# Talking-heads attention: three score tiles instead of two, values block by block with three head pairs an op, zero rows by transfer

## The chip, the cores and the metric

The kernel runs on one core of a Trainium2 chip. The metric is the device time of one execution in microseconds, as the median of several runs. Times inside an execution come from one profiled execution.

## What is computed

Attention over 4 batches, 12 heads, 448 positions and a head dimension of 64, in which the scores of all heads are mixed before the softmax and the weights after it; then two token-wise layers on the result. In short:

```python
scores = scale * np.matmul(q, k.transpose(0, 1, 3, 2))
scores = np.einsum('bhij,hg->bgij', scores, w_pre)
attn = softmax(scores)                      # over j
attn = np.einsum('bhij,hg->bgij', attn, w_post)
x = np.matmul(attn, v)                      # (4*448, 768) after a transpose
h = x @ w_in;  x = (h * np.cos(h)) @ w_out
h = np.maximum(np.maximum(x @ w1, x @ w2), x @ w3)
out = h @ w_out2
```

## The kernel before

The queries of a batch are cut into four **blocks** of 10, 12, 12 and 11 **slots** (the last batch in another order); a slot is 10 query rows, and the 12 heads of those 10 rows make 120 rows that the head mix works on. There are 16 blocks and 180 slots. A block goes through these steps (names and lines are those of the kernel before):

- **scores**: for each of the six head pairs, `qk` (L554) multiplies q and k of two heads on TensorE into two PSUM banks; `evac` (L462, the helper `copy`) copies each head's scores to SBUF, on ACT or DVE, into one of 7 places `s` (the first block uses places of `e` too).
- **regrouping**: `send` (L568) is one DMA a head, SBUF to SBUF, issued on SP. It spreads a head's 100 to 120 rows over the block's tile `t` (a *grid*), so that the 12 heads of a row come to lie on neighbouring partitions. There are two grids; block n uses grid `n % 2`, and a grid is free again when the block two earlier has been mixed. Four partitions of each grid are never written by a send and have to be zero; `fill` (L500) clears them with one GpSimd memset a grid.
- **mix and softmax**: a *visit* is two slots. `mix1` (L577) mixes heads on TensorE into two banks, `rowmax` (L585, DVE) and `soft` (L591, ACT) follow, then three small DVE steps, then `mix2` (L615) mixes the weights on TensorE into two banks of the pool `ps_t`, and `keep` (L462) copies each to the tile `a2`.
- **values**: blocks are grouped in **halves** (`HALVES`, L27): in batches 1 and 2 the halves are the blocks of 10 and 12 slots and those of 12 and 11; batches 0 and 3 have two halves of a single block and one of two. `av` (L641, L644) multiplies `a2` of a half with v, two head pairs an op, in one bank of `ps_t`; `keepx` (L462) copies each pair's part of each block to a tile `xs`, and `out` (L658) is one DMA a pair to `xT` in DRAM. `ps_t` has two banks, which mix2 and av share.

After attention the two layers run on TensorE (L158 to L160, three matmuls for each float32 product). Their input `x` (L141) is read back from `xT` into a tile of the same ring as the grids; the first few of their matmuls run between the last visits.

The order on every engine is fixed when the kernel is built: `Plan.run` (L392) takes the steps by modelled start time and rank, with modelled durations, rings of places and landing times. Each engine then works through its own list in that order; so does the SP queue with its DMAs.

```python
r = (first[n - 1] - 2.5 + 0.1 * score[n - 1][3] * hp) if n else -40.0 + hp   # L687: rank of block n's scores
```

Of the kernel before, what the change touches and what calls it, by code (L numbers as in the profile page):

```python
# [9 lines left out]
F32 = mybir.dt.float32  # L10
# [6 lines left out]
B, H, S, D = 4, 12, 448, 64  # L17
# [11 lines left out]
NHALF = 230  # L29
# [416 lines left out]
def attention(ctx, tc, q, k, v, w_pre, w_post, same_row, xT, tp, mlps):  # L446
# [34 lines left out]

    score, halves = [], []
    for b, sizes in enumerate(HALVES):
        i = 0
        for n, half in enumerate(sizes):
            start, column, nhalf = min(i, S - RI * half[0]), 0, len(halves)
            for slots in half:
                i = min(i, S - RI * slots)
                score.append((b, i, RI * slots, slots, nhalf, column))
                column += RH * slots  # L490
                i += RI * slots
            halves.append((b, start, i - start, 2 * column, range(len(score) - len(half), len(score))))
    visits = [(n, t, range(min(2, x[3] - t))) for n, x in enumerate(score) for t in range(0, x[3], 2)]
# [5 lines left out]
    def fill(n, _):  # L499
        nc.gpsimd.memset(grids[n][:PAD], 0.0)  # L500

# [64 lines left out]
    def send(n, h, eng):  # L566
        slots = score[n][3]
        queue_of[eng].dma_start(grids[n % 2][PAD + h:PAD + RI * H:H, :slots, :], live.pop(("s", n, h))[:RI * slots])  # L568

    def mix1(v, _):  # L570
        n, t, slots = visits[v]
        for a in range(2):
            live["m", v, a] = ps_m.tile([128, S], F32, name="mps")
        for y in slots:
            for a in range(2):
                k = slice(64 * a, PAD + (a + 1) * PH)
                nc.tensor.matmul(live["m", v, a][64 * y:64 * y + 64], w1[k], grids[n % 2][k, t + y, :],  # L577
                                 start=True, stop=True)
# [39 lines left out]
    def keep(v, y, eng):  # L618
        n, t, _ = visits[v]
        half, o = score[n][4], score[n][5] + RH * (t + y)  # L620
        if ("a2", half) not in live:
            live["a2", half] = ap_.tile([128, JB, H, NHALF // 2], F32, name="a2")
        copy(eng, live["a2", half][:, :, :, o:o + RH].rearrange("p u g r -> p (u g) r"),
             live["a", v, y].rearrange("p u (g r) -> p (u g) r", r=RH))


    def pairs(x):
        return 2 * x, 2 * x + 1

    def av(half, x, _):  # L630
        b, _, _, m, _ = halves[half]
        a2, w = live["a2", half], m // 2
        both = ps_t.tile([128, 512], F32, name="aps")
        for n, hp in enumerate(pairs(x)):
            ps = live["av", hp] = both[:, n * NHALF:n * NHALF + m].rearrange("p (a w) -> p a w", a=2)
# [10 lines left out]
    def keepx(half, hp, eng):  # L646

        xs = live["xs", hp] = xp.tile([128, NHALF], F32, name="xs")
        ps = live["av", hp]
        for n in halves[half][4]:  # L650
            _, i0, m, slots, _, c = score[n]
            o = i0 - halves[half][1]
            copy(eng, xs[:, o:o + m].rearrange("p (a r t) -> p a r t", a=2, t=slots),
                 ps[:, :, c:c + m // 2].rearrange("p a (t r) -> p a r t", r=RH))

    def out(half, hp, eng):
        b, i0, m = halves[half][:3]
        queue_of[eng].dma_start(xT[hp * 128:(hp + 1) * 128, b * S + i0:b * S + i0 + m], live["xs", hp][:, :m])  # L658

# [19 lines left out]
    for n in range(2):  # L679
        add(fill, (n,), -60.0, {"P": 5.0})  # L680
    add(wmix, (0,), -39.0, {"V": 0.8}, [("wget", 0), ("wget", 2)])
    add(wmix, (1,), -39.0, {"V": 0.2}, [("wget", 1), ("wget", 2)])
    for n in range(NS):
        b = score[n][0]
        start, end = score[n - 1][0] != b or not n, n == NS - 1 or score[n + 1][0] != b
        for hp in range(HP):
            r = (first[n - 1] - 2.5 + 0.1 * score[n - 1][3] * hp) if n else -40.0 + hp  # L687
            if start:
# [6 lines left out]
            for h in range(2 * hp, 2 * hp + 2):  # L695
                add(evac, (n, h), r, {"A": 0.42, "V": 0.53}, [("qk", n, hp)], turn=True, lands=0.16, takes=[place := copy_place(n, h)[0]], frees=[(ring, ("qk", n, hp), h % 2)])
                if h == 0:
                    plan.add(("new_t", n), r, lambda _: None, {}, [("evac", n, 0)], takes=["t"])
                add(send, (n, h), r, {"D": score[n][2] / 125.0}, [("evac", n, h), ("new_t", n)], turn=True, frees=[(place, ("evac", n, h))], lands=5.0)


    for y, (n, t, slots) in enumerate(visits):
# [12 lines left out]
        for c in slots:  # L715
            begin = n == halves[score[n][4]][4][0] and t == c == 0
            add(keep, (y, c), i + 1.5, {"A": 0.41, "V": 0.51}, [key("mix2")], turn=True, lands=0.17, takes=["a2"] * begin,
                frees=[("ps_t", key("mix2"), c)])


    for half, (b, _, _, _, members) in enumerate(halves):
        last = (first + [N])[members[-1] + 1] - 1
        ylast = starts[members[-1] + 1] - 1
        room = min(12, starts[halves[half + 1][4][-1] + 1] - 1 - ylast) if half + 1 < len(halves) else 12
        ends = [("keep", y, a) for y, x in enumerate(visits) if x[0] in members for a in x[2]]
        start = ends[0]
        for x in range(HP // 2):
            r = last + 2.5 + 3.0 * x
            for hp in pairs(x) if halves[half][1] == 0 else ():
                add(vget, (b, hp), r - 10.0, {"D": 0.8}, [("send", 0, H - 1)], turn=True, takes=["v"], lands=3.0)  # L730
            add(av, (half, x), r, {"T": 0.25 + 0.0139 * halves[half][3]}, [("vget", b, hp) for hp in pairs(x)] + ends, turn=True, takes=["ps_t"],
                frees=[("a2", start)] + [("v", ("vget", b, hp)) for hp in pairs(x) if halves[half][1] + halves[half][2] == S],
                behind=from_visit(ylast + 2 + x * room // 3))
            for hp in pairs(x):
                add(keepx, (half, hp), r, {"A": 0.13 * len(members), "V": 0.18 * len(members)}, [("av", half, x)], turn=True, lands=0.2,
                    takes=["xs"], frees=[("ps_t", ("av", half, x))])
                add(out, (half, hp), r, {"D": 0.5}, [("keepx", half, hp)], turn=True, frees=[("xs", ("keepx", half, hp))], lands=3.0)

# [207 lines left out]
    for n in range(2):  # L946
        r = (r0, N - 1)[n] + RANK[("fx", "x1")[n]]
        add(xget, (n,), r, {"D": 3.6}, [("out", x, hp) for x, y in enumerate(halves) if y[0] == n for hp in range(H // 2)] + [("xget", 0)] * n
            + [("block", FG)], takes=["t"])
# [36 lines left out]
    first_layer(0)  # L986
    plan.add(("open_late",), N, open_late, {}, [("keepx", len(halves) - 1, hp) for hp in range(HP)], behind=att_keys)
    for r, job in sorted(jobs):
# [118 lines left out]
    for u, (l, (j, wi)) in enumerate(units):  # L1107
# [72 lines left out]
    plan.run({**BUFS, "t": 2, "ps": BUFS["ps_x"], "mark": NM, "u": 7,  # L1180
              **{(tag, early): n if early else of - n for tag, (n, of) in PLACES.items() for early in (True, False)}})
# [45 lines left out]
```

## Time and profile before

| | us |
|---|---|
| median of 3 runs | 1140.23 (1139.26 to 1142.84) |
| the profiled execution's own time | 1143.35 |
| its span | 1141.5 |
| TensorE busy, share of the span | 97% |
| DVE busy, share of the span | 85% |
| ACT busy, share of the span | 58% |
| mean share of the 16 DMA engines' time, first 17 of 40 slices | 0.4 to 0.7 |

The steps below are measured against the profiled execution; its own time is 0.27% above the median. TensorE's records overlap, since matmuls are pipelined, so its busy share does not tell how close it is to its limit: what counts is the distance from the start of one group of matmuls to the start of the next. In a timeline row the columns are start, duration, engine, line, operation, `out<-in`, shapes and the count of merged instructions; in brackets stands the engine's idle time before it and what ended it.

### The profile page before, as it was taken

How to read it: one execution, taken by the hardware profiler on the slowest of the kernel's cores; microseconds unless marked ns; L12 is line 12 of the kernel's file. 1: busy time of each engine (PE TensorE's matmuls, PEld its weight loads, DVE VectorE, ACT ScalarE, POOL GpSimd, SP SyncE). 2: the span in 40 equal slices, each digit the busy share in tenths (PEclk: the TensorE clock that was granted, in tenths of full speed). 3: DMA queues.
4: the chain of work that ended last, by engine and by line, in shares of the span. 5: the costliest groups of instructions: out<-in, count | busy, mean ns of one | idle time of the engine just before them, and what ended most of it. 6: DMA issues, size and time to landing. Idle time of an engine off the chain costs nothing.

```text
span 1141.5 us, 28936 instructions
## 1 busy us (share of the span) xinstructions
PE 1112.7 (97%) x11548; PEld 936.5 (82%) x11548; DVE 974.8 (85%) x2060; ACT 661.9 (58%) x1493; POOL 76.7 (7%) x67
## 2 busy tenths in 40 slices
PE   7989999999998999999999999999999999999998
PEld 2556766676667899999999999999999999999987
DVE  4868677887978999999999999997987779778994
ACT  3757666667867885555555555555634354445572
POOL 4000000000023100000000000000001022011120
PEclk8999999999999999999999999999999999999999
DMA  7676685655554654434444444420012111222233
GB/s 227 199 221 199 207 218 158 203 179 155 167 181 139 200 153 139 138 118 131 126 128 128 130 116 125 130 89 22 1 56 76 63 49 41 77 64 69 85 121 113
DMA packets 92903, 146.79 MB, mean 129 GB/s; under 512 B 12288, under 2 KB 75360, under 8 KB 92768
## 3 DMA queue, kind: packets, MB, share of 16 engines
q1 hardware_dynamic: 92512, 144.92, 42.6%
q8 instruction: 91, 1.49, 0.5%
q14 instruction: 44, 0.36, 0.1%
q0 software_dynamic: 256, 0.02, 0.0%
HBM read 85.74 MB, written 20.45 MB: 93 GB/s over the span
## 4 chain that ended last, share of the span: by engine, by line
PE 86%; DMA 5%; DVE 4%; ACT 2%; issue 1%; SPq 1%; POOL 0%; ACTq 0%; DVEq 0%; POOLq 0%
PE ps L158 22%; PE ps L159 22%; PE ps L160 22%; PE aps L615 6%; PE mps L577 6%; PE ps L554 5%; PE aps L641 4%; DMA t<-s 2%; DMA x<-xT 1%; PE aps L644 1%; DMA k<-in_k_dram 1%; ACT e L591 1%; DMA xT<-xs 1%; DMA t<-e 1%; DVE nm L585 0%
## 5 line engine op out<-in xcount | busy, mean ns | idle before, releaser
L158 PE MATMUL ps<-x,w 128*128 128x448 f32 x816 | 300.0, 368 | 0.8 <-ACT gh L869 0.6
L160 PE MATMUL ps<-x,w 128*128 128x448 f32 x816 | 299.1, 367 | 0.3
L159 PE MATMUL ps<-x,w 128*128 128x448 f32 x816 | 299.1, 367 | 0.3 <-DVE w L298 0.3
L158 PEld LDWEIGHTS ps<-x,w 128*128 128x128 f32 x816 | 153.2, 188 | 15.3 <-ACT gh L869 1.0
L160 PEld LDWEIGHTS ps<-x,w 128*128 128x128 f32 x816 | 153.2, 188 | 14.9 <-POOL x L149 1.0
L159 PEld LDWEIGHTS ps<-x,w 128*128 128x128 f32 x816 | 153.2, 188 | 14.0 <-DVE w L298 0.7
L615 PEld LDWEIGHTS aps<-w2s,e 60*64 60x64 f32 x5040 | 103.7, 136 | 49.6 <-issue 25.9
L158 PE MATMUL ps<-gh,w 128*128 128x448 f32 x384 | 140.8, 367 | 0.0
L159 PE MATMUL ps<-gh,w 128*128 128x448 f32 x384 | 140.7, 366 | 0.0
L160 PE MATMUL ps<-gl,w 128*128 128x448 f32 x384 | 140.4, 366 | 0.0
L295 ACT CAST w<-wf 128x384 fp32r<-128x384 f32 x168 | 81.1, 514 | 77.5 <-DVE wf L287 55.8
L585 DVE TENSOR_REDUCE nm<-mps 128x1 f32<-128x448 f32 (+1 forms) x184 | 108.5, 615 | 20.3 <-PE mps L577 19.3
L591 ACT ACTIVATE e<-mps,nm 128x448 f32<-128x448 f32 (+1 forms) x184 | 116.3, 641 | 13.7 <-DVE nm L585 9.7
L615 PE MATMUL aps<-w2s,e 60*64 60x60 f32 x5040 | 105.4, 220 | 8.9 <-DVE xs L462 2.4
L554 PE MATMUL ps<-k,q 64*64 64x448 f32 (+3 forms) x736 | 101.0, 561 | 2.9 <-ACT s L462 2.7
L577 PE MATMUL mps<-t,w 64*64 64x448 f32 (+1 forms) x720 | 95.8, 567 | 7.3 <-DMA xT<-xs 4.6
L826 DVE TENSOR_TENSOR acc<-ps,acc 128x448 f32<-128x448 f32 x168 | 100.5, 617 | 0.6 <-PE ps L160 0.6
L298 DVE TENSOR_TENSOR w<-wf,w 128x384 fp32r<-128x384 f32 x132 | 75.3, 591 | 18.8 <-ACT w L295 18.0
L254 ACT ACTIVATE wf<-wraw 128x384 f32<-128x384 f32 x112 | 61.9, 554 | 48.9 <-DMA wraw<-in_w_out_dram 32.1
L298 POOL TENSOR_TENSOR w<-wf,w 128x384 fp32r<-128x384 f32 x36 | 43.6, 1217 | 674.4 <-DVE wt L258 365.1
L160 PEld LDWEIGHTS ps<-gl,w 128*128 128x128 f32 x384 | 72.1, 188 | 6.5
L158 PEld LDWEIGHTS ps<-gh,w 128*128 128x128 f32 x384 | 72.1, 188 | 6.3
(123 smaller groups left out, 1757.8 us busy)
## 6 DMA issues: line engine op xcount, KB each, us to landing
t<-s SPq DMA_DIRECT2D x96, 210.0 KB
wf<-w SPq DMA_DIRECT2D x96, 192.0 KB
wraw<-in_w_out_dram SPq DMA_DIRECT2D x44, 384.0 KB
wraw<-in_w_dram SPq DMA_DIRECT2D x36, 384.0 KB
wraw<-in_w_in_dram SPq DMA_DIRECT2D x32, 384.0 KB
t<-s SPq DMA_DIRECT2D x48, 192.5 KB
w<-wf SPq DMA_DIRECT2D x48, 192.0 KB
t<-s SPq DMA_DIRECT2D x42, 175.0 KB
```

The source lines that it names most:

```text
L158: mm(w[0], x[0], start=first, stop=False)
L159: mm(w[1], x[0], start=False, stop=False)
L160: mm(w[0], x[1], start=False, stop=last)
L254: nc.scalar.activation(o["f"], f32(o["raw"][:, :, 1]), AF.Abs)
L295: return nc.scalar.copy(A[x][0], w())
L298: return eng.tensor_sub(A[x][1], w(), f32(A[x][0]))
L554: nc.tensor.matmul(live["s", n, 2 * hp + g][r:end], live["q", b, hp][half, i0 + r:i0 + end], live["k", b, hp][half], start=True, stop=True)
L577: nc.tensor.matmul(live["m", v, a][64 * y:64 * y + 64], w1[k], grids[n % 2][k, t + y, :], start=True, stop=True)
L585: nc.vector.tensor_reduce(nm, of(v, live["m", v, a]), axis=AX.X, op=ALU.max, negate=True)
L591: nc.scalar.activation(of(v, e), of(v, live["m", v, a]), AF.Exp, bias=live["nm", v, a], scale=1.0, accum_out=live["z", v][:, a:a + 1])
L615: nc.tensor.matmul(live["a", v, y][64 * c:64 * c + 64, u], live["e", v, a][k, j * JC:j * JC + JC], live["w2s", v][k, a], start=True, stop= ...
L826: return nc.vector.tensor_add(acc, po, acc) if fg else nc.scalar.copy(acc, po)
```

## The change

- There are three grids; the third lies in the attention's constant pool. Block n uses grid n % 3, and the scores of block n get an earlier rank (8.0 instead of 2.5 steps ahead).
- `HALVES` is gone. `av` works on one block, three head pairs an op; `keepx` is one copy an op, of 300 to 360 columns, and `out` one DMA an op. `a2` and `xs` change their sizes; there are 9 places `s` instead of 7 and 3 larger `xs` instead of 6.
- `fill` is a DMA on ACT's queue from a small zeroed tile, one for each grid, instead of GpSimd memsets.
- In the first block the sends of heads 1, 4, 7 and 10 are issued on GpSimd's queue instead of SP's.
- The last batch's blocks have 12, 12, 11 and 10 slots.

```diff
-HALVES = [[[10], [12], [12, 11]], [[10, 12], [12, 11]], [[10, 12], [12, 11]], [[12, 11], [12], [10]]]
+SLOTS = [[10, 12, 12, 11]] * 3 + [[12, 12, 11, 10]]
+PG = 3
-BUFS = {"k": 10, "q": 9, "s": 7, "e": 6, "w2s": 3, "v": 7, "xs": 6, "a2": 2, "ps_m": 4, "ps_t": 2, "ps_x": 2}
+BUFS = {"k": 10, "q": 9, "s": 9, "e": 6, "w2s": 3, "v": 7, "xs": 3, "a2": 2, "t": 3, "ps_m": 4, "ps_t": 2, "ps_x": 2}
...
-    grids = [tp.tile([128, RT, S], F32, tag="t", name="t") for _ in range(2)]
+    grids = [const.tile([128, RT, S], F32, name="t")] + [tp.tile([128, RT, S], F32, tag="t", name="t") for _ in range(2)]
+    none = const.tile([PAD, S], F32, name="none")
+    nc.vector.memset(none, 0.0)
...
     def fill(n, _):
-        nc.gpsimd.memset(grids[n][:PAD], 0.0)
+        nc.scalar.dma_start(grids[n][:PAD], none[:PAD].unsqueeze(1).to_broadcast([PAD, RT, S]))
...
-    def av(half, x, _):
+    def av(n, x, _):
+        b, _, m, _ = score[n]
+        a2, w = live["a2", n], m // 2
+        live["av", n, x] = ps_t.tile([128, 512], F32, name="aps")[:, :PG * m]
+        for y, hp in enumerate(group(x)):
+            ps = live["av", n, x][:, y * m:y * m + m].rearrange("p (a w) -> p a w", a=2)
...
+    def keepx(n, x, eng):
+        m, slots = score[n][2:]
+        xs = live["xs", n, x] = xp.tile([128, PG * RT * RI], F32, name="xs")[:, :PG * m]
+        copy(eng, xs.rearrange("p (a r t) -> p a r t", r=RH, t=slots),
+             live["av", n, x].rearrange("p (a t r) -> p a r t", r=RH, t=slots))
...
-            r = (first[n - 1] - 2.5 + 0.1 * score[n - 1][3] * hp) if n else -40.0 + hp
+            r = (first[n - 1] - 8.0 + 0.1 * score[n - 1][3] * hp) if n else -40.0 + hp
...
-                add(send, (n, h), r, {"D": score[n][2] / 125.0}, ..., lands=5.0)
+                add(send, (n, h), r, {"P": 0.6} if n == 0 and h % 3 == 1 else {"D": score[n][2] / 125.0}, ..., lands=7.0)
```

How the instructions move, in three places. First ACT's list at the start of the program (a number behind a name tells tiles apart; brackets give the semaphores that a row waits for, DMAHW those of DMAs). Before:

```order
L462 ACT_TABLE_LOAD
L462 COPY s_179<-ps_170 100x448 [waits PE_49]
L462 COPY s_193<-aps_185 100x448 [waits PE_49]
L462 COPY s_207<-mps_199 100x448 [waits PE_49]
L462 COPY s_222<-ps_212 100x448 [waits PE_49]
```

and with the change:

```order
L500 DMA t_136<-none_139 4x12x448 [waits DVE_49]
L500 DMA t_137<-none_139 4x12x448 [waits DMAHW5_49]
L500 DMA t_138<-none_139 4x12x448 [waits DMAHW6_49]
L464 ACT_TABLE_LOAD
L464 COPY s_184<-ps_176 100x448 [waits PE_49]
```

Three DMAs now stand ahead of ACT's first copy, and two of them wait for a DMA's semaphore, the ones of the third pair's q and k.

Second, SP's list of DMAs where the first block's sends end. Before:

```order
L568 DMA t<-e 10x10x448
L568 DMA t<-s 10x12x448 x8
L539 DMA v_126<-in_v_dram 64x512 x2
L568 DMA t<-s 10x12x448 x2
L539 DMA v_127<-in_v_dram 64x512 x2
```

and with the change:

```order
L568 DMA t<-e 10x10x448 x2
L568 DMA t<-s 10x12x448 x10
L539 DMA v_126<-in_v_dram 64x512 x2
L568 DMA t<-s 10x12x448 x2
L539 DMA v_127<-in_v_dram 64x512 x2
L539 DMA v_128<-in_v_dram 64x512 x2
L568 DMA t<-s 10x12x448 x6
```

Ten instead of eight sends of the second block (10x12x448) stand ahead of the first loads of v, and six of the third block's follow before the other three loads of v.

Third, PE's list where the values of a block of 12 slots follow a visit. Before, in the half of 12 and 11 slots of batch 0:

```order
L577 MATMUL mps<-t,w_124 64x448 x4
L641 MATMUL aps<-a_1251,v_126 64x230 x6
L644 MATMUL aps<-a_1251,v_126 64x115 x4
L641 MATMUL aps<-a_1251,v_127 64x230 x6
L644 MATMUL aps<-a_1251,v_127 64x115 x4
L641 MATMUL aps<-a_1251,v_128 64x230 x6
L644 MATMUL aps<-a_1251,v_128 64x115 x4
L641 MATMUL aps<-a_1251,v_129 64x230 x6
L644 MATMUL aps<-a_1251,v_129 64x115 x4
L554 MATMUL ps<-k,q 64x448 x2
```

and with the change, the last three of the six head pairs of the block of 12 slots:

```order
L640 MATMUL aps<-a_1266,v_129 64x120 x6
L643 MATMUL aps<-a_1266,v_129 64x60 x4
L640 MATMUL aps<-a_1266,v_130 64x120 x6
L643 MATMUL aps<-a_1266,v_130 64x60 x4
L640 MATMUL aps<-a_1266,v_131 64x120 x6
L643 MATMUL aps<-a_1266,v_131 64x60 x4
L554 MATMUL ps<-k,q 64x448 x2
L554 MATMUL ps<-k,q 56x448 x2
L615 MATMUL aps<-w2s,e 64x60 x28
```

The rows of a head pair are as many as before and half as wide, and all six pairs of the block come in a row.

## Rows read from the trace of the kernel before

**Rows 1.** Busy time by stretch; columns as in the first line.

```profile
core 0: us, PE busy (x) PEld busy (x) DVE busy (x) ACT busy (x) POOL busy (x), PEclk, DMA share, GB/s
24.00:112.00 88.00, 82.20 (x1986) 51.51 (x1987) 70.00 (x186) 58.99 (x161) 0.00 (x0) 0.93 0.73 207
112.00:192.00 80.00, 77.32 (x1873) 54.71 (x1872) 62.95 (x174) 53.37 (x150) 0.00 (x0) 1.00 0.68 195
192.00:272.00 80.00, 77.96 (x1880) 54.08 (x1872) 64.09 (x177) 53.82 (x151) 0.00 (x0) 1.00 0.60 180
272.00:363.00 91.00, 84.55 (x1960) 62.91 (x1956) 73.48 (x182) 62.90 (x169) 14.86 (x13) 1.00 0.54 162
363.00:1141.00 778.00, 773.52 (x3784) 708.88 (x3781) 692.53 (x1325) 424.40 (x851) 48.33 (x40) 1.00 0.34 101
```

**Rows 2.** Timeline of PE, one visit after another in batch 1.

```profile
121.28 1.02 PE L577 MATMUL mps<-t,w 64*64 64x448 f32 x8
...
123.60 1.01 PE L577 MATMUL mps<-t,w 64*64 64x448 f32 x8
```

**Rows 3.** Timeline of PE, values: two neighbouring head pairs at each width.

```profile
113.55 1.34 PE L641 MATMUL aps<-a,v 128*64 128x230 f32 x12
...
115.11 1.34 PE L641 MATMUL aps<-a,v 128*64 128x230 f32 x12
...
338.48 0.80 PE L641 MATMUL aps<-a,v 128*64 128x120 f32 x12
...
339.33 0.80 PE L641 MATMUL aps<-a,v 128*64 128x120 f32 x12
...
44.76 0.76 PE L641 MATMUL aps<-a,v 128*64 128x100 f32 x12
...
45.54 0.72 PE L641 MATMUL aps<-a,v 128*64 128x100 f32 x12
```

**Rows 4.** Timeline of PE, waits within the attention.

```profile
119.76 0.97 PE L615 MATMUL aps<-w2s,e 60*64 60x60 f32 x50 [0.34 <-DVE xs L462]
...
78.08 1.27 PE L554 MATMUL ps<-k,q 64*64 64x448 f32 x8
82.08 1.77 PE L577 MATMUL mps<-t,w 64*64 64x448 f32 x8 [2.74 <-DMA xT<-xs]
...
164.58 0.98 PE L577 MATMUL mps<-t,w 64*64 64x448 f32 x8 [1.82 <-DMA xT<-xs]
```

**Rows 5.** Busy time by stretch of 4 us, columns as in rows 1.

```profile
4.00:8.00 4.00, 3.45 (x18) 0.83 (x16) 2.18 (x4) 0.53 (x1) 4.00 (x5) 1.00 0.96 291
...
20.00:24.00 4.00, 2.56 (x8) 0.28 (x6) 0.00 (x0) 1.06 (x2) 0.00 (x0) 0.50 0.66 205
...
84.00:88.00 4.00, 4.00 (x68) 2.08 (x64) 2.54 (x6) 2.27 (x6) 0.00 (x0) 0.50 0.78 215
```

**Rows 6.** Timeline of all engines, the start of the program.

```profile
1.29 1.20 POOL L510 DMA_DIRECT2D wraw<-in_w_pre_dram  x2 [0.83 <-DVE blk L473]
...
6.54 0.53 ACT L462 COPY s<-ps 100x448 f32<-100x448 f32 x1 [4.51 <-PE ps L554]
...
8.24 0.56 PEld L554 LDWEIGHTS mps<-k,q 64*64 64x64 f32 x8 [0.93 <-DMA q<-in_q_dram]
...
10.63 4.02 DVE L516 TENSOR_SCALAR wraw<-wraw 128x12 f32<-128x12 f32 x1
...
17.53 0.76 SPq L568 DMA_DIRECT2D t<-e  x1
...
24.10 3.27 PE L577 MATMUL mps<-t,w 64*64 64x448 f32 x16 [1.14 <-DMA t<-e]
```

**Rows 7.** Chain of waits, start and length, where the first layer's input is read back.

```profile
320.82 8.56 DMA x<-xT
```

**Rows 8.** Groups of copies on ACT, by shape.

```profile
L462 ACT COPY a<-aps 128x420 f32<-128x420 f32 x94 | 52.7, 563 | 37.2 <-PE aps L615 35.4
...
L462 ACT COPY xs<-aps 128x120 f32<-128x120 f32 x26 | 6.6, 263 | 30.1 <-PE aps L644 30.1
```

More of the change, by code (lines that the diff above doesn't have):

```diff
@@ L479, in attention @@
         nc.tensor.matmul(begun[:64], w1[:64], places[0][:64].rearrange("p j g d -> p (j g d)")[:, :S], start=True, stop=True)
-    score, halves = [], []
-    for b, sizes in enumerate(HALVES):
+    score = []
+    for b, sizes in enumerate(SLOTS):
         i = 0
[L485 to L492, printed above, removed]
+        for slots in sizes:
+            i = min(i, S - RI * slots)
+            score.append((b, i, RI * slots, slots))
+            i += RI * slots
     visits = [(n, t, range(min(2, x[3] - t))) for n, x in enumerate(score) for t in range(0, x[3], 2)]
@@ L619, in keep, with group @@
         n, t, _ = visits[v]
[L620 to L623, printed above, removed]
+        if ("a2", n) not in live:
+            live["a2", n] = ap_.tile([128, JB, H, RT * RH], F32, name="a2")
+        copy(eng, live["a2", n][:, :, :, RH * (t + y):RH * (t + y + 1)].rearrange("p u g r -> p (u g) r"),
              live["a", v, y].rearrange("p u (g r) -> p (u g) r", r=RH))
-    def pairs(x):
-        return 2 * x, 2 * x + 1
-    def av(half, x, _):
[L631 to L635, printed above, removed]
+    def group(x):
+        return range(PG * x, PG * x + PG)
+    def av(n, x, _):
[4 more added lines that the diff above has]
+            ps = live["av", n, x][:, y * m:y * m + m].rearrange("p (a w) -> p a w", a=2)
             for j in (*range(1, JP + 1), 0, JP + 1):
@@ L644, in av, with out @@
                         nc.tensor.matmul(to[:, a], of, rows[:, 2 * JP], start=False, stop=j > 0)
[L646 to L658, printed above, removed]
+    def keepx(n, x, eng):
[3 more added lines that the diff above has]
+             live["av", n, x].rearrange("p (a t r) -> p a r t", r=RH, t=slots))
+    def out(n, x, eng):
+        b, i0, m, _ = score[n]
+        known = max(0, sum(score[n - 1][1:3]) - i0) if n and score[n - 1][0] == b else 0
+        to = xT.rearrange("(c p) t -> p c t", p=128)[:, PG * x:PG * x + PG, b * S + i0 + known:b * S + i0 + m]
+        queue_of[eng].dma_start(to, live["xs", n, x].rearrange("p (c m) -> p c m", m=m)[:, :, known:])
     before = {}
@@ L715, in attention @@
         for c in slots:
-            begin = n == halves[score[n][4]][4][0] and t == c == 0
-            add(keep, (y, c), i + 1.5, {"A": 0.41, "V": 0.51}, [key("mix2")], turn=True, lands=0.17, takes=["a2"] * begin,
+            add(keep, (y, c), i + 1.5, {"A": 0.41, "V": 0.51}, [key("mix2")], turn=True, lands=0.17, takes=["a2"] * (t == c == 0),
                 frees=[("ps_t", key("mix2"), c)])
[L721 to L729, printed above, removed]
-                add(vget, (b, hp), r - 10.0, {"D": 0.8}, [("send", 0, H - 1)], turn=True, takes=["v"], lands=3.0)
[L731 to L737, printed above, removed]
@@ new lines, in attention @@
+    for n, (b, i0, m, slots) in enumerate(score):
+        last = (first + [N])[n + 1] - 1
+        ylast = starts[n + 1] - 1
+        ends = [("keep", y, a) for y, x in enumerate(visits) if x[0] == n for a in x[2]]
+        for x in range(HP // PG):
+            r = last + 2.5 + 4.0 * x
+            for hp in group(x) if i0 == 0 else ():
+                add(vget, (b, hp), r - 10.0, {"D": 0.8}, [("send", 0, H - 1)], turn=True, takes=["v"], lands=3.0)
+            add(av, (n, x), r, {"T": 0.3 + 0.0209 * m}, [("vget", b, hp) for hp in group(x)] + ends, turn=True, takes=["ps_t"],
+                frees=[("a2", ends[0])] + [("v", ("vget", b, hp)) for hp in group(x) if i0 + m == S],
+                behind=from_visit(ylast + 2 + 3 * x))
+            add(keepx, (n, x), r, {"A": 0.1 + 0.0025 * m, "V": 0.08 + 0.003125 * m}, [("av", n, x)], turn=True, lands=0.2,
+                takes=["xs"], frees=[("ps_t", ("av", n, x))])
+            add(out, (n, x), r, {"D": 0.5}, [("keepx", n, x)], turn=True, frees=[("xs", ("keepx", n, x))], lands=3.0)
@@ L947, in attention @@
         r = (r0, N - 1)[n] + RANK[("fx", "x1")[n]]
-        add(xget, (n,), r, {"D": 3.6}, [("out", x, hp) for x, y in enumerate(halves) if y[0] == n for hp in range(H // 2)] + [("xget", 0)] * n
+        add(xget, (n,), r, {"D": 3.6}, [("out", x, y) for x, of in enumerate(score) if of[0] == n for y in range(HP // PG)] + [("xget", 0)] * n
             + [("block", FG)], takes=["t"])
```

15 lines of the change are left out of this document (7 added, 8 removed).

## Prediction

> **What bounds the kernel now.** I read the stretches first, then PE's timeline, then the waits. From 363 us on PE runs the two layers: 773.5 of 778 us busy with 3784 matmuls, 0.204 us each [rows 1]. The changed order has the same 3780 product matmuls in a row there, so this part stays, and the change is worth what it does between 24 and 363 us.
>
> There, busy time tells little; pitches do. A visit (one mix, one score pair, one weight mix) takes 123.60 - 121.28 = 2.32 us from one mix to the next when PE waits for nothing [rows 2], a third of it (0.77) for each. A head pair's values take 115.11 - 113.55 = 1.56 us at 230 columns, 0.85 at 120 and 0.78 at 100 [rows 3]; for 220 I take 1.50 in proportion. A batch has 22.5 visits, 1.5 score pairs more than visits, and two halves of six head pairs: 52.2 + 1.2 + 6 x (1.56 + 1.50) = 71.8 us of work for PE. The stretches of batches 1 and 2, which begin at the same point of their batches, are 80 us long [rows 1], so 8.2 us of each are lost. The first stretch holds, by the order of before, 23.5 full visits, four mixes and 2.5 score pairs more, and twelve narrow head pairs: 54.5 + 4.9 + 9.8 = 69.2 of 88 us; 18.8 are lost. The last one (the whole, 288.2 us of work, less the other three, 36 product matmuls among it) has 75.4 of 91; 15.6 are lost. PE's work is thus 85% of the attention, and 51 us are waits, half clock and switches.
>
> Where they are: mixes that wait for the sends of their block (2.74 us idle at 82.08, and 82.08 - 78.08 - 0.77 = 3.2 us in all; 1.82 at 164.58 [rows 4]; the record named is a DMA to xT, but the mix reads t, and its last send shares that DMA's semaphore); PE at half clock, granted 0.50 at 84 to 88 us after that wait and at 20 to 24 us before the first mix [rows 5]; and weight mixes that wait for a bank while four copies to xs follow each other after a wide op (0.34 us at 119.76 [rows 4], seven such).
>
> **The change, part by part.**
>
> *Third grid, earlier scores, 9 places s.* A send needs about 0.6 us of copy, 0.76 us of issue [rows 6] and, judging by the first block (issued at 17.53, mixed at 24.10 [rows 6]), some 6 us to land: 8 us from the last score to the first mix. Counted in the orders, PE has between the last score pair and the first mix of block 3 two mixes, two weight mixes, three score pairs and four value pairs before: 8.8 us of work. With the change it has six, five, five and six: 17.5 us. So 8.8 us just covers the landing and 17.5 covers it twice. The waits for sends should go: 1.8 us in batch 1 [rows 4]. In the first stretch 18.8 us are lost where batches 1 and 2 would lose 8.2 x 88/80 = 9.0; of the 9.8 above that I leave 3 us, the half clock right after the first mix (about 6 us of work at half speed [rows 5]), and take 6.8 away: the wait at 82.08, the 3 us that its half clock costs, and small ones. What is late next is ACT and DVE: together 116 us busy per 80 us [rows 1], 73% each, if shared evenly.
>
> *Values block by block.* Six wide halves become twelve narrow blocks; all 16 blocks are narrow then: four of 100, four of 110 (0.815, between the others), eight of 120 columns. 6 x (4 x 0.78 + 4 x 0.815 + 8 x 0.85) = 79.1 us against 6 x (4 x 1.56 + 2 x 1.50 + 2 x 0.78 + 2 x 0.85) = 75.0: **+4.1 us**, all on PE. The number of ops hardly changes, 32 for 30.
>
> *One copy an op.* 96 copies of about 0.26 us become 32 of 360 columns or less; between 120 columns (263 ns) and 420 (563 ns) [rows 8] that is 0.5 us. ACT and DVE lose some 9 us of work between them, hidden behind PE. On PE's path is the chain of four copies after a wide op; with one copy of 0.5 us behind a score pair of 0.77 us the bank is free in time: 7 x 0.34 = **-2.4 us**. If the copy queues behind others on its engine, this stays; bounds 0 and -2.4.
>
> *32 DMAs to xT instead of 60*, of rows half as long: nobody waits for them but the read of x. Taken as nothing.
>
> *The read of x.* It waits for the tile of the block two earlier before, and is on the chain with 8.56 us [rows 7]; ACT stands in its list at the cast of x until it lands, and copies for PE queue behind that. With three grids the tile is that of block 13, free a block earlier. The last stretch loses 15.6 us where 9.3 would be usual; bounds 0 and -6.3, and I take **-3**, since that stretch also has no scores left to fill PE, which stays.
>
> *The beginning.* Three things that the trace does not show together. SP issues 8 sends instead of 12 at 0.76 us or more, and both GpSimd memsets go, in whose time a DVE step on 12 columns took 4.02 us [rows 6] with two heads' copies behind it: up to 4 x 0.76 = 3 us earlier. Against it, ACT now has three DMAs ahead of its first copy, the last two behind the landing of the third pair's q and k; PE had waited for that until 8.24, while the first copy began at 6.54 [rows 6]. So ACT begins some 2 to 3.5 us later. And four sends go through GpSimd, whose nearest DMAs, of 60 short rows, took 0.6 us each to issue [rows 6]. Bounds -3 and +3.5; I take 0, as the two large parts are equal and opposite. The second of them is a price of the three zero rows only: 258 KB at 291 GB/s [rows 5] would be 0.9 us.
>
> On that price the row and a rule differ. While q and k were loaded, the DMA engines were 0.96 busy and moved 291 GB/s; with the sends alone in flight, 0.66 and 205 GB/s [rows 5], although PE was waiting for them. The Trainium skill (DMA: Bandwidth & Descriptors, "Why a DMA increments its semaphore by 16 and not by 1") says that a transfer is spread over the largest number of engines up to 16 that divides its outermost dimension: 10 for a send, 4 for a fill. The 0.66, near 10/16, agrees. By that rule the fills take 258 KB at a quarter of 291 GB/s, 3.5 us of four engines that every send also uses, and the sum would be 3 us higher.
>
> *Sum:* -1.8 - 6.8 + 4.1 - 2.4 - 3 + 0 = **-9.9 us**. The profiled execution took 1143.35 us, so 1133.4; it stood 0.27% above the median of 1140.23, against which I forecast **1130**. The bounds of these terms alone give 1124 to 1137.
>
> **The rivals.**
>
> *More than that goes.* If the long lead also empties ACT's and DVE's queues at the right times, batches 1 and 2 lose half (4 us each), the start comes 3 us earlier and the first half clock with it. For: within the visits PE runs at 2.32 us without a gap. Against: 73% of two engines in fixed order seldom leaves no gaps. 1130 - 8 - 6 = 1116.
>
> *The sends do not get ahead.* Scores wait in s until sent; if DMAs with q, k and v of two batches in the same queue limit the first stretch (share 0.73 there [rows 1]), its 6.8 us stay. For: 0.96 at the start. Against: 0.60 to 0.68 in batches 1 and 2. 1137. This is also the case that the change does not do what it says.
>
> *The waits move.* PE is held back by ACT and DVE whichever grid is ready: 51 us stay lost, and the narrow values cost 4.1, the copies give 2.4: 1142.
>
> *A late beginning: slower.* The first mix needs all twelve heads. If the fills hold ACT, its copies hold PE's banks, and the four GpSimd sends are slow to write out (100 rows of 448 values where the trace has 60 of 12), the first mix comes late one for one, and PE idles at half clock meanwhile. From a first mix at 34 us on, 10 us late, the gain is eaten; four sends of 4 us each behind a first copy at 10 us, with 6 us to land, would put it at 32 and the half clock makes it worse. At 44 us it is 1150. For: three DMAs ahead of ACT's copies. Against: 0.6 us an issue.
>
> **How the numbers follow.** A measurement of this kernel tells 0.3%, 3.4 us, from no change. Forecast 0.52 (1124 to 1135); more 0.20 (1112 to 1124); sends not ahead 0.13 (1135 to 1139, half of it faster than the bound); waits move 0.08; late beginning 0.07. Faster 0.80, same 0.13, slower 0.07. For 8 in 10 I leave out the lower end of the second case and the last two but for their edge: 1115 to 1139.
>
> **What would show it.** First mix between 21 and 28 us. No mix of batches 0 to 2 that waits for a send by over 1 us, and no half clock between 35 and 350 us. Value pairs at 0.78 to 0.85 us, copies to xs near 0.5 us, no weight mix waiting for them. x landed before ACT needs it. The end of the attention near 353 us and the rest of 778 us unchanged. I am wrong if the first mix is past 30, if the first batch still takes 88 us, or if batches 1 and 2 take 80 us or more: then ACT and DVE bound them.

## The result

The change made the kernel slower: 1159.41 us (median of four, 1156.19 to 1162.49) against 1139.89 on the same chip, ratio 1.014 (95%: 1.010 to 1.018). The forecast was 1130, with a range of 1115 to 1139. The profiled execution took 1158.15 us, span 1156.0, beside 1143.35 and 1141.5 before.

Busy time by stretch of the changed kernel, columns as in [rows 1]; the last two lines are eight microseconds each of the layers:

```profile
24.00:112.00 88.00, 77.56 (x1734) 50.75 (x1736) 54.78 (x145) 52.79 (x137) 0.00 (x0) 0.91 0.74 217
112.00:192.00 80.00, 78.39 (x2130) 59.30 (x2128) 62.02 (x165) 55.14 (x145) 0.00 (x0) 1.00 0.70 201
192.00:272.00 80.00, 78.86 (x2130) 60.88 (x2126) 57.43 (x156) 57.01 (x153) 0.00 (x0) 1.00 0.62 184
372.17:1156.00 783.83, 776.48 (x3781) 711.01 (x3780) 693.04 (x1322) 423.44 (x847) 49.08 (x41) 1.00 0.33 100
388.00:396.00 8.00, 5.52 (x19) 3.87 (x18) 7.86 (x12) 6.87 (x16) 3.64 (x4) 0.76 0.32 85
396.00:404.00 8.00, 8.00 (x34) 7.26 (x33) 7.97 (x14) 5.50 (x13) 1.62 (x2) 0.81 0.39 118
```

The first stretch has 77.6 us of PE where it had 82.2 [rows 1]; the two whole batches after it are a little fuller. Three points divide the span: the first mix (24.10 before, 31.54 after), the end of the last values (363.15, 372.17) and the end. The 14.5 us of the two spans are +7.4 before the first mix, +1.6 from there to the end of the attention, where the forecast had nearly all its gain, and +5.5 in the layers, where it had nothing.

The beginning, timeline of ACT and PE of the changed kernel:

```profile
1.49 9.79 ACTq L500 DMA_DIRECT2D t<-none  x3
...
12.60 0.53 ACT L464 COPY s<-ps 100x448 f32<-100x448 f32 x1
...
18.25 0.97 PE L554 MATMUL mps<-k,q 64*64 64x448 f32 x8 [1.82 <-DMA k<-in_k_dram]
...
31.54 2.84 PE L577 MATMUL mps<-t,w 64*64 64x448 f32 x16
```

ACT is held for 9.79 us at its three DMAs of zero rows (the second and third wait for the third pair's q and k) and copies from 12.60 on (6.54 before [rows 6]), and a score of block 0 still waits for its k until 18.25. The chain of waits shows why that k is late. With the change it has the first DMA of zero rows, for whose landing a load of k in SP's list waits, and then the last k of block 0:

```profile
1.49 6.80 DMA t<-none
...
9.16 8.96 DMA k<-in_k_dram
```

Before, loads of k stand there, and the last of them on the chain lands 12.6 us after the start:

```profile
2.13 4.75 DMA k<-in_k_dram
6.90 5.72 DMA k<-in_k_dram
```

The first batch, SP's own list, then what waits for it:

```profile
82.11 3.35 SPq L568 DMA_DIRECT2D t<-s  x4
85.51 2.35 SPq L539 DMA_DIRECT2D v<-in_v_dram  x2
...
92.60 2.17 SPq L529 DMA_DIRECT2D k<-in_k_dram  x1
94.86 3.48 SPq L568 DMA_DIRECT2D t<-s  x4
...
100.42 0.62 DVE L464 COPY s<-ps 120x448 f32<-120x448 f32 x1 [7.00 <-DMA t<-s]
...
101.10 1.00 PE L554 MATMUL ps<-k,q 64*64 64x448 f32 x3 [6.54 <-DVE s L464]
```

No mix waits there for more than 0.6 us any more. A score pair of the next block does: its copy needs a place s, the places are full until sends leave, and 9 us of loads and writes (85.51 to 94.86) stand between two sets of sends in SP's list. PE idles 6.54 us and then runs at half clock (0.50 granted from 100 to 104).

The start of the layers, waits on PE's timeline:

```profile
390.05 0.47 PE L162 MATMUL ps<-x,w 128*128 128x448 f32 x1 [0.80 <-DVE x L151]
...
392.51 0.74 PE L160 MATMUL ps<-x,w 128*128 128x448 f32 x1 [1.38 <-ACT x L147]
...
393.91 0.74 PE L162 MATMUL ps<-x,w 128*128 128x448 f32 x1 [0.29 <-POOL x L151]
```

PE waits 2.5 us for the parts of x of the third quarter of the tokens, and the mean granted clock falls to 0.76 and 0.81 for two stretches of 8 us (3.4 us of work). Before, the same place has three short pauses (0.44 to 0.49 us from one start to the next, where 0.2 is usual) and full clock:

```profile
379.00:387.00 8.00, 7.69 (x36) 6.20 (x35) 7.93 (x15) 6.74 (x16) 2.44 (x2) 1.00 0.38 103
387.00:395.00 8.00, 8.00 (x41) 7.41 (x40) 7.97 (x14) 7.15 (x17) 2.30 (x2) 1.00 0.42 127
```

A fourth kind of wait was nearly absent before. PE stops in the middle of a weight mix, for nothing that the profile shows:

```profile
154.37 0.99 PE L615 MATMUL aps<-w2s,e 60*64 60x60 f32 x49
...
156.98 0.34 PE L615 MATMUL aps<-w2s,e 60*64 60x60 f32 x7 [1.61 <-issue]
```

It runs 49 of 56 matmuls, then comes a gap, then the other 7. Such gaps of 0.4 us or more add up to 6.0 us in the attention, 1.2 before.

### The profile page after: what moved, and what is told of

Same layout as the page of the kernel before. It is cut to its first block, busy times and chain, and to the rows that moved or that the text cites. A ratio compares the mean times of both kernels' runs of the same rounds, so it can differ in the third digit from the quotient of the medians.

```text
span 1156.0 us, 30223 instructions
## 1 busy us (share of the span) xinstructions
PE 1119.8 (97%) x12268; PEld 958.2 (83%) x12268; DVE 960.1 (83%) x2012; ACT 667.9 (58%) x1479; POOL 69.0 (6%) x68
## 4 chain that ended last, share of the span: by engine, by line
PE 89%; DMA 5%; DVE 2%; ACT 2%; issue 1%; SPq 1%; POOL 0%; DVEq 0%; POOLq 0%; ACTq 0%
PE ps L160 22%; PE ps L161 22%; PE ps L162 22%; PE aps L615 6%; PE mps L577 6%; PE ps L554 5%; PE aps L640 5%; DMA t<-s 2%; PE aps L643 2%; DMA v<-in_v_dram 1%; DMA k<-in_k_dram 1%; DMA t<-none 1%; DMA wraw<-in_w_in_dram 0%; DVE x L151 0%; POOL x L151 0%
## 5 line engine op out<-in xcount | busy, mean ns | idle before, releaser
L615 PEld LDWEIGHTS aps<-w2s,e 60*64 60x64 f32 x5040 | 107.5, 135 | 40.8 <-issue 14.3
L591 ACT ACTIVATE e<-mps,nm 128x448 f32<-128x448 f32 (+1 forms) x184 | 117.2, 649 | 20.4 <-DVE nm L585 18.3
L585 DVE TENSOR_REDUCE nm<-mps 128x1 f32<-128x448 f32 (+1 forms) x184 | 108.6, 613 | 12.1 <-PE mps L577 11.2
L554 PE MATMUL ps<-k,q 64*64 64x448 f32 (+3 forms) x736 | 105.8, 572 | 10.5 <-DVE s L464 6.5
L464 DVE COPY s<-ps 120x448 f32<-120x448 f32 (+2 forms) x82 | 49.7, 619 | 64.0 <-PE ps L554 51.7
L577 PE MATMUL mps<-t,w 64*64 64x448 f32 (+1 forms) x720 | 99.9, 555 | 1.3 <-issue 0.6
```

The source lines that it names most:

```text
L554: nc.tensor.matmul(live["s", n, 2 * hp + g][r:end], live["q", b, hp][half, i0 + r:i0 + end], live["k", b, hp][half], start=True, stop=True)
L585: nc.vector.tensor_reduce(nm, of(v, live["m", v, a]), axis=AX.X, op=ALU.max, negate=True)
L591: nc.scalar.activation(of(v, e), of(v, live["m", v, a]), AF.Exp, bias=live["nm", v, a], scale=1.0, accum_out=live["z", v][:, a:a + 1])
L615: nc.tensor.matmul(live["a", v, y][64 * c:64 * c + 64, u], live["e", v, a][k, j * JC:j * JC + JC], live["w2s", v][k, a], start=True, stop= ...
```

## The experiments

All runs are in one table. It gives the ratio to the kernel before on the same chip (95% interval; where there is one run alone, its time and before's median) and, from one profile each and in us, the start of the first mix, the end of the attention, the time from there to the end (layers) and the sum of PE's gaps without visible cause in the attention. Ten runs of one kernel (e1) spread over 1143.9 to 1154.8, so a difference of a few us between two single profiles proves nothing by itself.

| kernel | ratio | first mix | attention ends | layers | gaps |
|---|---|---|---|---|---|
| before | 1 | 24.1 | 363.2 | 778.4 | 1.2 |
| changed | 1.014 (1.010–1.018) | 31.5 | 372.2 | 783.8 | 6.0 |
| e1 old beginning | 1.0046 (1.0013–1.0080) | 26.3 | 364.1 | 782.3 | 6.5 |
| e2 before, new beginning | 1.0067 (1.0031–1.0103) | 27.7 | 368.4 | 779.4 | 1.9 |
| e3 old fills, new sends | 1.0061 (1.0027–1.0094) | 29.7 | 364.8 | 781.8 | 5.2 |
| e4 before, values by block | 1.0090 (1.0058–1.0123) | 21.5 | 368.1 | 787.2 | 11.2 |
| e5 DMA fills, old sends | 1153.2 / 1145.4 | 31.3 | 370.0 | 781.3 | 7.5 |
| e6 e1, late cuts on DVE | 1.0055 (1.0030–1.0080) | 26.1 | 362.1 | 784.0 | 3.5 |
| e7 e6, rank 2.5 | 1.0099 (1.0067–1.0131) | 21.7 | 368.6 | 785.3 | 9.8 |
| e8 e6, rank 5 | 1.0090 (1.0063–1.0118) | 25.8 | 367.7 | 782.7 | 7.4 |
| e9 e1, loads behind sends | 1.0105 (1.0079–1.0132) | 21.9 | 366.1 | 784.1 | 3.5 |
| e10 fills on GpSimd's queue | 1157.7 / 1144.9 | 35.1 | 375.1 | 780.7 | 5.0 |
| e11 e1, two pairs an op | 1157.2 / 1144.9 | 23.7 | 370.5 | 784.9 | 5.1 |
| e12 e9, rank 12 | 1.0162 (1.0137–1.0187) | 26.2 | 380.8 | 782.5 | 5.6 |
| e13 before, values split | 1.0019 (0.9996–1.0042) | 21.7 | 370.3 | 778.4 | 2.4 |
| e14 before, WAIT 0.05 | 1.0077 (1.0046–1.0109) | 23.8 | 368.5 | 782.7 | 0.4 |
| e15 e1, WAIT 0.05 | 1.0066 (1.0033–1.0099) | 23.5 | 361.8 | 783.8 | 11.2 |
| e16 e1, WAIT 0.02 | 1.0100 (1.0046–1.0154) | 23.6 | 373.1 | 786.5 | 14.4 |
| e17 before, WAIT 0.02 | 1.0040 (1.0016–1.0065) | 23.1 | 369.2 | 783.6 | 0.5 |
| e18 before, rank 3 | 1.0000 (0.9978–1.0021) | 21.4 | 363.2 | 778.6 | 2.5 |

### The beginning: e1, e2, e3, e5, e10

e1, the changed kernel without its new beginning:

```diff
-        nc.scalar.dma_start(grids[n][:PAD], none[:PAD].unsqueeze(1).to_broadcast([PAD, RT, S]))
+        nc.gpsimd.memset(grids[n][:PAD], 0.0)
-    add(send, (n, h), r, {"P": 0.6} if n == 0 and h % 3 == 1 else {"D": ...
+    add(send, (n, h), r, {"D": ...
```

> The changed kernel with the old beginning: zero rows by GpSimd memsets, all sends of the first block on SP. Theory (the new beginning delays the first mix): the first mix returns from 31.5 to 24 to 25 us, the end of the attention from 372.1 to 364 to 366, and the time from 1159 to 1152 +- 3. Rival (the delay belongs to the third grid and the 18 values ops, or is made up for later): first mix at 24, but the attention still ends past 369 and the time stays over 1155. The stall of PE at 94 us, which theory puts to loads standing ahead of the sends in SP's list, is to stay in either case.

The first mix came at 26.34, the attention ended at 364.05, and the time was 1150.08 us: this is the theory, though the first mix is 1.3 us later than it said. The stall stayed (2.89 us at 91.86).

e2, the same two edits the other way on the kernel before (with two fills).

> The kernel before with nothing but the new beginning (zero rows by DMAs on ACT's queue, four sends of the first block on GpSimd; two grids, two halves a values op). Theory: first mix from 24.1 to 30 to 32 us, the time up by 5 to 8 to about 1146. Rival (it needs the third fill to hurt): first mix at 24 to 27, time within 3 us of before.

The first mix is 3.6 us later (27.69), the end of the attention 5.3, and the ratio is 1.0067, 7 us: less than expected at the start, as much as expected in the time.

e3, only the fills back to memsets:

> The changed kernel with GpSimd memsets for the zero rows, but the four sends of the first block still on GpSimd. Theory A (the fills hold ACT's queue until 11.3 us and the loads behind them): first mix 24 to 26, as in the run with the whole old beginning. Theory B (GpSimd's sends are the slow part): first mix 28 or later. If both count, between: 26 to 28.

The first mix came at 29.66, which is theory B's figure. But the GpSimd sends stood behind three memsets here (13.6 us, until 19.2), so the first mix decides for neither theory. The attention ends at 364.82, only 0.8 us after e1's: from the first mix on it takes 335.2 us, e1 337.7.

e5, the other half: DMA fills, all sends on SP.

> The changed kernel with its DMAs of zero rows on ACT's queue, but all sends of the first block on SP as before. Theory (the fills hold ACT, and the loads of q and k behind them in the shared places of the DMA queues): first copy of ACT again at 12 to 13 us, last scores of block 0 at 17 to 19, first mix 29 to 32. Rival (the sends on GpSimd were the slow part): first mix 26 to 27.

The fills alone put the first mix at 31.28, and the attention ends 6.0 us after e1's. The time of this one run (1153.2) lies within the spread of e1's ten and tells nothing. ACT and PE of e5:

```profile
1.49 9.84 ACTq L500 DMA_DIRECT2D t<-none  x3
...
12.65 0.53 ACT L464 COPY s<-ps 100x448 f32<-100x448 f32 x1
...
31.28 3.26 PE L577 MATMUL mps<-t,w 64*64 64x448 f32 x16 [1.28 <-issue]
```

e10, fills issued by GpSimd, sends on SP: `nc.scalar.dma_start(grids...` becomes `nc.gpsimd.dma_start(grids...`.

> The changed kernel with all sends of the first block on SP and its DMAs of zero rows issued by GpSimd instead of ACT. Theory (what costs is that ACT's queue stands until a fill's place in the hardware queues is free, and that loads wait for the fills' places): ACT's first copy back at 6.5 to 7, last scores of block 0 at 13 to 15, first mix 25 to 27. Rival (the transfers themselves take the DMA engines from the loads, whoever issues them): loads of q and k land late all the same, first mix 29 or later.

```profile
5.64 1.88 POOL L500 DMA_DIRECT2D t<-none  x3
...
6.45 0.33 SPq L529 DMA_DIRECT2D k<-in_k_dram  x1
...
7.00 0.53 ACT L464 COPY s<-ps 100x448 f32<-100x448 f32 x1 [4.97 <-PE ps L554]
...
8.64 8.77 SPq L568 DMA_DIRECT2D t<-e  x1
...
17.70 1.76 PE L554 MATMUL aps<-k,q 64*64 64x448 f32 x8 [7.33 <-DMA k<-in_k_dram]
...
35.11 3.62 PE L577 MATMUL mps<-t,w 64*64 64x448 f32 x16
```

The rival won. ACT is free at 7.00 and the last load of q and k was issued at 6.45, yet PE waits for one k until 17.70 and for the next until 21.41, where the last such wait ended at 18.25 with the fills on ACT's queue. So the transfers cost, not ACT's list alone. The trace's DMA records show them: the 144 packets of 1792 bytes of the changed kernel's three fills took 0.27 us in the median, where a packet of that size on SP's queue takes 0.074 to 0.079 us in the first 28 us of the kernel before; in e10 the fills have packets of 5376 bytes at 1.7 us.

### Values by block, and PE's instructions: e4, e11, e13

e4, the kernel before with the changed values, copies and writes only.

> The kernel before with nothing but the values block by block (three pairs of heads an op, one copy, one write): two grids, 7 places s, the scores where they were, the old beginning. By the terms on record: PE +4.1 us for narrower outputs, -2.4 us for the copies: 1142, between 1138 and 1146; the waits on sends at 82 us and between 112 and 192 us stay. Rival (the third grid was there only to pay for what block-by-block values lose): 1148 or more. Rival (the values are the whole gain of the steady batches): under 1138, with batches of 79 us.

The ratio is 1.0090, 10 us, where the terms on record gave 2; the time is in the range of the first rival (1148 or more). The waits of mixes for sends, which were to stay, nearly went, though there are two grids (0.96 us at 58.00 and 0.60 at 144.6 are left). The layers take 787.2 us, and PE's gaps without visible cause add up to 11.2 us, the largest of them:

```profile
332.44 0.56 PE L613 MATMUL aps<-w2s,e 60*64 60x60 f32 x20
335.68 0.74 PE L613 MATMUL aps<-w2s,e 60*64 60x60 f32 x35 [2.67 <-issue]
```

What they wait for shows in the DMA records. Of the 97 such gaps in the table's 20 profiles, 95 end 1.2 to 1.7 us after a 16 KB packet of queue q8 has landed, where a moment taken at random would do so about one time in ten. The page of the profile names the queue's kind (queue, packets, MB, share), before and then changed:

```profile
q8 instruction: 91, 1.49, 0.5%
```

```profile
q8 instruction: 96, 1.57, 0.6%
```

The two traces hold 23245 and 24677 records of PE's matmuls and weight loads, 255 and 257 for each packet. So PE waits for its own instructions.

e13, as many instructions as e4 on the kernel before, order as it was:

```diff
-    nc.tensor.matmul(to, of, rows[:, 2 * j - 2:2 * j], start=j == 1, stop=False)
+    for a in range(2):
+        nc.tensor.matmul(to[:, a], of, rows[:, 2 * j - 2 + a], start=j == 1 and a == 0, stop=False)
```

> The kernel before with each first matmul of the values (two slots' columns, 200 to 230 wide) split into two of half the columns: as many columns, 720 more matmuls and weight loads on TensorE, every other engine's order as it was. Theory (TensorE waits for its own instructions when they follow each other too fast): gaps without a visible cause of 0.4 us or more add up to 4 to 11 us where the kernel before had 1.2, each ending 1.3 to 1.7 us after a packet of the instruction queue landed; time up by 3 to 9 us. Rival (the gaps come with the blocks' structure, its copies and places in PSUM): they stay at 1 to 2 us and the time within 2 us of before.

It has 96 packets too, but gaps of 2.4 us and a ratio of 1.0019, whose interval holds no change. Both figures lie between the theory and its rival, far below e4's: the number of instructions alone is not the cause. (Its profile, with the attention's end at 370.3, is of the longest of its ten runs.)

e11, `PG = 2` in place of 3 on e1 (with the planner's times for it, and the casts' rank of e9):

> Values block by block with two pairs of heads an op (three ops a block of 80 matmuls instead of two of 120), old beginning, scores 8 mixes ahead, early casts of x. TensorE has as many instructions, in shorter bursts. Theory (the issue gaps of TensorE come where its instructions follow each other fastest, a run of values and second mixes): the gaps of 0.4 us or more add up to under 4 us where three pairs an op had 5 to 7 (11 with two grids). Rival (they follow the number of instructions): 5 to 7 us again.

The gaps are 5.1 us, the rival's figure, so shorter runs of values did not help in this one profile. All kernels with values by block have 3.5 to 14.4 us of gaps, all with halves 0.4 to 2.5; why the blocks make them stays open.

### The lead of the scores: e7, e8, e9, e12

e7 and e8: `first[n - 1] - 8.0` becomes `- 2.5` and `- 5.0`, on e6 (below).

> As the run before it, but the scores of the next block stand where they stood in the kernel before (2.5 mixes ahead of the block before instead of 8), so that third grid and places are there, but are not used earlier by order. Theory (the stall of scores on places s at 92 us comes from the earlier scores: the loads of the next batch's q and k move ahead with them and stand in front of the sends in SP's list): no wait of scores on a copy of over 1 us between 85 and 105, the attention ends 1 to 3 us earlier than in that run. Rival (the earlier scores are what the third grid is for): waits of mixes on sends as in the kernel before come back (2 to 4 us in all), and the attention ends later by as much.

> As the run with late cuts on VectorE, but scores 5 instead of 8 mixes ahead. Theory: between the two, the stall at 92 us under 1.5 us, no mix waits for a send; 1143 to 1147. Rival: the issue gaps of TensorE (5 to 7 us with values by block, 1 to 2 in the kernel before) stay whatever the rank is, and so does a time above the kernel before.

With 2.5 the stall is gone and waits of mixes come back (2.15 us at 56.99 for t, 1.51 at 80.56): the rival of e7. With 5 one of 2.14 comes back at 163.57, against the theory of e8, and the time is 5 us above its range; the gaps stay at 7.4, as its rival said. The attention ends at 368.6 and 367.7, and at 362.1 with 8; the median times are 1155.6, 1152.2 and 1150.2. So the early scores help, but how much they are worth by themselves is not shown, since PE's gaps differ as well (9.8, 7.4 and 3.5 us).

e9, loads of q and k planned behind the block before's sends, and casts of x for later quarters at an earlier rank:

```diff
-    add(kget, (b, hp), r - early, ..., lands=2.5)
+    add(kget, (b, hp), r - early, ..., lands=2.5, behind=[("send", n - 1, H - 1)] if n else [])
-            r = base(n) - 3.0 + c * 0.4
+            r = base(n) - 9.0 + c * 0.1
```

> Old beginning, three grids, scores 8 mixes ahead, and two edits of order: the loads of a batch's q and k wait in the plan until the sends of the block before are issued, and the casts of x for the third and fourth quarter of the tokens get an earlier rank (9 instead of 3 before their products). Theory 1 (sends stand behind loads in SP's list): no wait of scores on a copy of over 1 us between 85 and 105, clock in 24:112 at 0.97 or more, the attention ends at 357 to 361 instead of 364. Theory 2 (the sixth cast of the third quarter's x stands behind other work in ACT's list): from there to the end 779 +- 1 instead of 782 to 784. Together 1139 to 1143 beside 1145 for the kernel before. Rivals: the stall moves to another wait, attention end 363 or more; the layers stay at 782 or more, because the read of x itself is late.

Both theories fell. The stall at 92 went, but scores now wait for loads, and the attention ends at 366.1 instead of 357 to 361. On e9's PE:

```profile
68.97 1.68 PE L552 MATMUL ps<-k,q 64*64 64x448 f32 x8 [4.30 <-DMA k<-in_k_dram]
...
151.20 1.72 PE L552 MATMUL ps<-k,q 64*64 64x448 f32 x7 [3.40 <-DMA k<-in_k_dram]
```

The layers took 784.1 us, with a wait of 4.16 us for gh, an input of the next product, in place of those for x.

e12, rank 12 on e9:

> As the first run of this set with the scores 12 mixes ahead instead of 8. Since 2.5, 5 and 8 gave ends of the attention at 368.6, 367.7 and 362 to 364, theory (a longer lead takes away what is left of waits on sends) expects the same or up to 2 us less; rival (places s are full, the scores block TensorE ahead of mixes): 2 us more or worse, with waits of scores on copies.

It is worse, as the rival said: the attention ends at 380.8. But the scores wait for loads of k, for up to 6.57 us, and not for copies.

### What an order costs: e6, e14 to e18

e6, on e1: `{"P": 1.15, "V": 0.535}` of the late low parts of x becomes `{"V": 0.535}`.

> The old beginning with three grids, and the low parts of x of the third and fourth quarter of the tokens on VectorE alone instead of VectorE or GpSimd. Theory (GpSimd's cuts of x just after the attention slow VectorE's operations beside them, ACT waits for one of those and its sixth cast comes late): from the end of the attention to the end of the program 782.3 falls to 779 +- 1, TensorE keeps its full clock there, the time 1146 to 1148 where the run with the old beginning had 1150.1. Rival (the block of layers is longer for another reason, x read later for instance): 782 or more.

The layers take 784.0 us, with 1.93 us of waiting for DVE's cut: the theory fell.

e14, on the kernel before: `WAIT = 0.034` becomes `0.05`. Same work, same tiles, another order.

> The kernel before with the planner's constant WAIT at 0.05 instead of 0.034: the same work in another order. Theory (the time from the end of the attention on, 778.4, belongs to an order for which the ranks were set, and any other order is worse): 781 to 785 there, and a time 2 to 8 us above before. Rival (values by block make the layers' start longer): 778 to 779.5, and a time within 2 us of before.

The ratio is 1.0077, 9 us, a little more than the theory's 2 to 8. The layers take 782.7 us, and the waits of e14's PE at their start look like the changed kernel's:

```profile
386.52 0.47 PE L160 MATMUL ps<-x,w 128*128 128x448 f32 x1 [0.60 <-POOL x L149]
...
387.74 0.47 PE L160 MATMUL ps<-x,w 128*128 128x448 f32 x1 [0.34 <-POOL x L149]
...
390.17 0.48 PE L160 MATMUL ps<-x,w 128*128 128x448 f32 x1 [1.54 <-DVE x L149]
```

e15 and e16, WAIT at 0.05 and 0.02 on e1:

> The changed kernel with the old beginning and WAIT at 0.05: another order of the same work. Theory (order): the end of the attention and the layers move by some us either way, 1146 to 1156. Rival (values by block): layers again 782 or more and the time at 1150 +- 2.

> The changed kernel with the old beginning and WAIT at 0.02: as the run before, a second sample of order. 1146 to 1156; if one of the two is under 1143, the third grid pays with an order of its own.

The ratios are 1.0066 and 1.0100 (e16's 1156.5 us is just past its range); no order tried brought the changed work below the kernel before.

e17, WAIT at 0.02, and e18, `- 2.5` becomes `- 3.0`, both on the kernel before:

> The kernel before with WAIT at 0.02 instead of 0.034: a second sample of order with the same work. Theory (its ranks were set for its own order): 2 to 10 us above before, from the end of the attention on 780 to 785. Rival (e14 was one bad sample): within 3 us of before, 778 to 779.5.

> The kernel before with the scores 3.0 instead of 2.5 mixes ahead: a small change of order in the attention, ACT's list of the layers as before. Theory: 778 to 779.5 from the end of the attention on, and a time within 3 us of before. Rival (any other order in the attention costs as well): layers as before, time 3 us or more above before.

The ratios are 1.0040 with layers of 783.6 us, and 1.0000 with 778.6. ACT's list of the layers is that of the kernel before, word for word, in e2 and e18, whose layers take 779.4 and 778.6 us; where it differs (e14, e17) they take 4 to 5 us more, with no other edit. All kernels with the changed work have another list, and 780.7 to 787.2 us. So the layers' 5.5 us need no other cause than the order, into which values, grids and x enter only through the planner.

## Why the prediction was wrong

PE's lost time shows best which steps failed. Priced as the forecast priced it, PE's work from the first mix to the end of the attention is 287.4 us before and 290.7 with the change (an estimate from the counts of matmuls in the two traces). That leaves 51.6 and 49.9 us lost, where the terms other than the values wanted 14.0 us back. By batches, each with a quarter of the mixes:

| us lost | batch 0 | batch 1 | batch 2 | batch 3 |
|---|---|---|---|---|
| before | 18.2 | 8.9 | 8.2 | 16.3 |
| changed | 18.8 | 6.4 | 6.4 | 18.3 |

The gain of the middle batches came; those of the first (-6.8) and the last (-3) did not. In the first batch the stall for a place s takes 6.5 us; over all four the gaps take 4.8 us more than before. The rest of the longer time is the late beginning and the layers. Point by point, by the forecast's own steps:

- **"So this part stays"** (the layers) failed: +5.5 us. The same products stood in PE's list, but the planner had put ACT's and DVE's lists beside them in another order, and the forecast looked at PE's alone. e14 and e17, beside e18, show that such an order alone makes 4 to 5 us.
- **The beginning, "I take 0"** failed: +7.4 us to the first mix, about 8 (372.2 - 364.1) at the end of the attention, more than twice its upper bound of 3.5. The price of "258 KB at 291 GB/s", 0.9 us, was taken for transfers whose packets took 0.27 us in the median, over three times a load's of the same size. By the rule of the Trainium skill that is cited there (DMA: Bandwidth & Descriptors, "Why a DMA increments its semaphore by 16 and not by 1") the sum would have been 3 us higher, by an estimate. That, too, was short of what e1 and e5 show, 5 to 8 us. The gain of DVE did come (the 4.02 us step takes 0.16) and was worth nothing, since the sends were late. The rival of the late beginning had this mechanism, with fills that hold ACT, and its sign, a first mix past 30; its other part, slow GpSimd sends, cost little (the attention of e3 ends 0.8 us after e1's).
- **Third grid, earlier scores**: right in that mixes of the attention no longer wait for sends, the 2.74 and 1.82 us of [rows 4]. In all eleven kernels with three grids and scores 8 or 12 steps ahead no mix behind the first waits over 0.6 us for a DMA; in the six with two grids and halves such waits of 0.5 us or more add up to 4 to 10 us. How much of that is the third grid's is not shown, since e4 with two grids has 1.6. Wrong was "what is late next is ACT and DVE": next is SP, whose list has loads in front of sends, and PE waited 6.54 us for a place s and ran at half clock again. The first batch, -6.8 in the sum, gained nothing.
- **Values block by block, +4.1**: PE's own work is near it (0.75, 0.80 and 0.85 us a head pair, where 0.78, 0.815 and 0.85 were taken). Missing was PE's wait for instructions, 6.0 us where there were 1.2.
- **One copy an op, -2.4**: the size was right, the gain not whole. The changed kernel's group of copies on ACT:

```profile
L464 ACT COPY xs<-aps 128x360 f32<-128x360 f32 x14 | 6.4, 459 | 28.7 <-PE aps L643 25.8 <-DMA xT<-xs 2.9
```

  A copy takes 459 ns where 0.5 us was taken, but the second values op now waits for the copy of the first (three waits, 1.7 us in all).
- **The read of x, -3**: it left the chain of waits as forecast, and DVE took its place. Part of the changed kernel's chain where the read had been:

```profile
350.73 1.15 DVE x L151 x2
351.88 0.28 DVE wt L260
...
352.19 0.56 DVE wt L264
352.75 1.50 DVE x L151
354.24 1.43 DVE wt L268
```

  The last batch lost 18.3 us, 3.2 of them in gaps without visible cause, where it had lost 16.3 and no such gaps. Nothing came of the -3; of its "bounds 0 and -6.3" the 0 was nearer.
- **"The bounds of these terms alone give 1124 to 1137"** has a slip: with the copies at their bound of 0 the slow end is 1139.

The largest fault lies over all of them: a sum of terms of 2 to 7 us was made for a program whose order a planner makes anew, while a mere constant of that planner moves its time by 0.4 to 0.8% (e14, e17). The range held no such term. The changed work with the old beginning is at 1.0046 to 1.0100 over three values of WAIT, the old work in other orders at 1.0000 (e18), 1.0040 and 1.0077: apart from its beginning, the change can't be told from a change of order by its time, though it can by its gaps.

## What to carry to other kernels

Where a planner orders all engines, run the old kernel with slightly different constants first: what that costs, here 0 to 0.8%, an edit can cost by its order alone, and it goes into the range on the slow side. When waits on one queue are removed by working further ahead, read that queue's whole list, since the next wait may be for what now stands in front. And price a new transfer by a row of the same kind, or not at all: three fills of four partitions each moved the end of the attention by 6 us here (e5 beside e1).

## What the runs showed of the hardware

- PE can wait for its own instructions: a gap inside a run of equal matmuls, ended 1.2 to 1.7 us after a 16 KB packet of its instruction queue landed (95 of 97 gaps).
- Zero rows copied to four partitions moved at 0.27 us (median) for a packet of 1792 bytes, while a packet of that size on SP's queue took 0.074 to 0.079 us in the kernel before.
- PE's mean granted clock was 0.76 in the 8 us from 388, in which it waited 0.80, 1.38 and 0.29 us, and 0.81 in the next 8 us; from 404 to 412 it was 1.00 again. In the kernel before, with pauses of 0.44 to 0.49 us from one start to the next at the same place, it stayed at 1.00.
